# GpSimd's semaphore waits for VectorE extended to the additions of token sums and weights

## The chip, the cores and the metric

One core of one Trainium2 chip runs the kernel. The metric is the device time of one execution in microseconds (us). The engines are TensorE (PE, with PEld for its weight loads), VectorE (DVE), ScalarE (ACT), GpSimd (POOL) and SyncE (SP), which issues nearly all DMAs.

## The reference

Attention with a mask, followed by two dense layers (all fp32):

```python
q_bucket = hash(q @ proj > 0); k_bucket = hash(k @ proj > 0)      # 6 bits each
mask   = q_bucket[:, None] == k_bucket[None, :]
scores = where(mask, q @ k.T / sqrt(64), -1e9)                    # batch 2, 8 heads, 768 tokens
attn   = exp(scores - max); attn = attn / (sum(attn) + 1e-9)
x = (attn @ v).transpose(...).reshape(1536, 512)
x = mish(x @ w_in1) @ w_out1                                      # 512 -> 2048 -> 512
h = x @ w_in2
out = (h - tanh(h)) @ w_out2
```

The four weight arrays come as float64 words and are converted to fp32 on the chip.

## The kernel before

**Precision.** Each fp32 matrix is split into a high and a low fp32r part (a copy, then a subtraction), and a product is three products of the parts. A large share of the work on ScalarE, VectorE and GpSimd is this splitting.

**Attention** takes about the first 230 us. It goes over eight pairs of heads; a pair has four rounds (two heads, two halves of the tokens) of six column chunks. Per round TensorE makes scores into PSUM, VectorE takes the minimum and clamps (line 672), ScalarE makes the exponential (line 694), TensorE transposes the weights back into PSUM (lines 734 and 736), and each transposed chunk is split into `ph` and `pl`: most by ScalarE and VectorE straight from PSUM (lines 757 and 763), some by GpSimd from a copy that ScalarE puts into SBUF (line 749; lines 750 and 753, the former shown in the profile as line 421, the helper `pool_copy`). TensorE then multiplies by the values (lines 706 and 709). Beside this run, for the next pair, the splitting of q, k and v (lines 472, 503 and 627, with the copies on line 421) on GpSimd, the hash bits on VectorE (line 508, two halves in each pair), and the DMAs that stack operands. `finish` (lines 822 to 829) scales the result of a pair and puts it into `xh` and `xl`.

**Dense layers.** Each is eight units of 256 hidden columns over two blocks of tokens. Most units use a seven-product block scheme (Strassen's kind) that needs sums and differences of token blocks (`tokens`) and of weight blocks. For the first block the raw sums are made of attention's results in the fp32 tiles that the results were written to; the differences among them are made by `diff` (line 1026), on VectorE, and can run during attention, as soon as two pairs are finished. The weights of the first two units are converted during attention as well (`to_float`: lines 954 and 962 on VectorE, line 970 on ScalarE, line 974 on GpSimd).

**Order of issue.** Every instruction group is an `op` with an engine, a cost and a key. `Plan.order` (lines 235 on) simulates the engines with these costs and sorts all groups by their planned start; the program is written out in that order, and each engine executes its own instructions in order. The planner counts a VectorE group as `inside` when its cost is over 0.3 and none of its buffers lies in PSUM (line 231). It never plans such a group beside a GpSimd group. When the program is written out, a semaphore wait repeats a part of this on the chip:

```python
    holders = []                                                   # line 1547
    for o in plan.order():
        made = o.fn()
        if o.eng == "DVE" and plan.inside(o) and made is not None:
            holders.append(made)
        elif o.eng == "POOL" and made is not None:
            for h in holders[-1:]:
                tc.add_manual_dep(made.ins, h.ins.name, ..., reason="port")
            holders.clear()
```

So a GpSimd group waits for the last `inside` VectorE group written out since the GpSimd group before it, if that VectorE group's function returned its instruction. The functions for lines 954 and 962 do. Those that call `add` (line 919; its instruction is line 920) return nothing, since `add` returns nothing. `add` makes the token differences (line 1026), the low parts of the split token blocks (1037) and weights (1113 and 1119), the weight sums (1103 to 1106) and most of VectorE's work in the dense layers. GpSimd has no work after attention.

Of the kernel before, what the change touches and what calls it, by code (L numbers as in the profile page):

```python
# [32 lines left out]
ALU = mybir.AluOpType  # L33
# [288 lines left out]
def tile_lsh_attention_moe(  # L322
# [34 lines left out]
    op, buf, room = plan.op, plan.buf, plan.room  # L357
# [559 lines left out]
    dram = {}  # L917

    def add(eng, out, in0, in1, sub=False):
        eng.tensor_tensor(out=out, in0=in0, in1=in1, op=ALU.subtract if sub else ALU.add)  # L920

    def unit_at(n):
        return T_MOE + n * UNIT
# [73 lines left out]
    def tokens(layer, sb, keys, slack):  # L997
# [11 lines left out]
        for k in range(2):  # L1009
# [10 lines left out]
            def whole(name, i, key, k=k, x=x, tmp=tmp, both=both):  # L1020
                at_ = ops[name][0]
                if (layer, sb) != (1, 0):
                    op(*TOKS, key, lambda: add(et, tmp(i), at_(0, k), at_(1, k)), [*x_of(name), *gate], both(i), release=key - slack)

            def diff(i, a, b, key, x=x, tmp=tmp, both=both):
                op(*TOKS, key, lambda: add(et, tmp(i), tmp(a), tmp(b), True), [*both(a), *both(b)], both(i))

            def place(name, i, key, k=k, x=x, tmp=tmp, both=both):
                at_ = ops[name][0]
                if name == "t1":  # L1030
                    toks = x_of("b12")
                    hi, lo = toks[:HT], toks[HT:]
                else:
                    (h, l) = more[("t2", "t3", "t4").index(name)]
                    hi, lo = [(h, k)], [(l, k)]
                op("ACT", 0.38, key, lambda: nc.scalar.copy(at_(0, k), tmp(i)), [*both(i), *gate], hi)
                op("DVE", 0.48, key + 0.1, lambda: add(nc.vector, at_(1, k), tmp(i), at_(0, k), True), [*both(i), *hi], lo)
# [576 lines left out]
```

## Time and profile before

| what | value |
| --- | --- |
| median of 3 runs | 739.85 us (739.48 to 739.94) |
| profiled execution, device time | 739.25 us |
| its span, first to last instruction | 737.5 us |
| TensorE, matmuls busy | 717.1 us (97%) |
| VectorE busy | 647.6 us (88%) |
| ScalarE busy | 508.8 us (69%) |
| GpSimd busy | 181.8 us (25%) |
| mean granted TensorE clock | 0.993 |

Busy time is summed over the whole span, so the stages differ from these shares: GpSimd's 181.8 us all lie in the first 230. Times in the profile count from the first instruction of the span. "Idle before" is the time in which an engine did nothing before an instruction, and the name behind it is the instruction that ended the wait.

### The profile page before, as it was taken

To read this page: it belongs to the slowest core of one execution; us is meant where nothing else is said; L and a number is where in the kernel's file an instruction comes from. 1 tells how busy PE (TensorE), PEld (TensorE's weight loads), DVE (VectorE), ACT (ScalarE), POOL (GpSimd) and SP (SyncE) were. 2 spreads that over 40 slices of the span, in tenths; PEclk is the share of its full clock that TensorE was granted. 3 is DMA by queue.
4 is the path that set the end of the run, shared out by engine and by line. 5 is a ranking of instruction groups with operands and counts; after the bars stand their busy time and mean duration, and the time that the engine had idled before them with its cause. 6 is when DMAs were issued, how large, how long until landed. Compare 5 with 4: busy or idle time off the path is not lost.

```text
span 737.5 us, 12852 instructions
## 1 busy us (share of the span) xinstructions
PE 717.1 (97%) x4381; PEld 656.0 (89%) x4381; DVE 647.6 (88%) x1348; ACT 508.8 (69%) x1093; POOL 181.8 (25%) x245
## 2 busy tenths in 40 slices
PE   8995999999999999999999999999999999999998
PEld 5784898888888998999999999999999899999998
DVE  7999999999999999998798998789999575767883
ACT  5994898999995966676576666676666345476660
POOL 6797599989950000000000000000000000000000
PEclk9997999999999999999999999999999999999999
DMA  8884568686651665556544754999876786745621
GB/s 216 201 219 113 151 171 211 171 217 170 135 186 25 232 194 172 175 198 224 205 171 144 253 208 174 363 362 326 326 282 251 279 272 241 229 156 189 212 97 64
DMA packets 60673, 150.87 MB, mean 205 GB/s; under 512 B 7256, under 2 KB 23768, under 8 KB 60608
## 3 DMA queue, kind: packets, MB, share of 16 engines
q1 hardware_dynamic: 60320, 149.75, 62.8%
q8 instruction: 34, 0.56, 0.3%
q10 hardware_dynamic: 288, 0.30, 0.2%
q14 instruction: 31, 0.25, 0.1%
HBM read 88.19 MB, written 43.04 MB: 178 GB/s over the span
## 4 chain that ended last, share of the span: by engine, by line
PE 73%; DVE 17%; issue 4%; ACT 3%; POOL 1%; DMA 1%; SPq 0%; DVEq 0%; POOLq 0%; ACTq 0%
PE pt L1152 10%; PE pt L1154 10%; PE pt L1153 10%; PE pt L1242 6%; DVE p L672 6%; PE pt L1230 5%; PE pt L1229 5%; PE s L1229 5%; PE pt L1468 5%; PE s L1468 3%; PE s L1242 3%; DVE pl L763 2%; PE pt L736 2%; PE pt L709 2%; PE pt L706 2%
## 5 line engine op out<-in xcount | busy, mean ns | idle before, releaser
L694 ACT ACTIVATE p<-p,mn 128x768 f32<-128x768 f32 x96 | 91.1, 949 | 17.8 <-DVE p L672 15.9
L1152 PE MATMUL pt<-xh,a 128*128 128x384 f32 x280 | 94.3, 337 | 0.4 <-DVE ph L920 0.4
L1154 PE MATMUL pt<-xh,a 128*128 128x384 f32 x280 | 94.4, 337 | 0.0
L1153 PE MATMUL pt<-xl,a 128*128 128x384 f32 x280 | 94.4, 337 | 0.0
L763 DVE TENSOR_TENSOR pl<-pt,ph 128x384 fp32r<-128x384 f32 x148 | 77.4, 548 | 1.2 <-ACT ph L757 0.2
L757 ACT CAST ph<-pt 128x384 fp32r<-128x384 f32 x148 | 68.2, 486 | 8.0 <-PE pt L736 6.4
L1230 PE MATMUL pt<-gh,o 128*128 128x256 f32 x256 | 71.9, 281 | 0.0
L736 PE MATMUL pt<-idr,split 128*128 128x128 f32 x544 | 68.6, 241 | 0.2 <-DVE pl L763 0.2
L736 PEld LDWEIGHTS pt<-idr,split 128*128 128x128 f32 x544 | 62.3, 141 | 5.7 <-DVE p L672 0.4
L709 PE MATMUL pt<-pl,vt 128*64 128x384 f32 x192 | 66.2, 348 | 0.1
L706 PE MATMUL pt<-ph,vt 128*128 128x384 f32 x192 | 66.0, 345 | 0.0
L920 DVE TENSOR_TENSOR gl<-pl,gh 128x384 fp32r<-128x384 f32 x96 | 52.4, 553 | 10.1 <-ACT gh L1176 9.8
L672 DVE TENSOR_SCALAR_CACHE_REDUCE p<-s 128x768 f32<-128x768 f32 x62 | 58.7, 947 | 2.1 <-PE s L669 1.9
L668 PE MATMUL s<-b,a 128*128 128x512 f32 x124 | 45.5, 367 | 11.2 <-DVE p L672 10.9
L1152 PEld LDWEIGHTS pt<-xh,a 128*128 128x128 f32 x280 | 52.6, 188 | 3.8 <-DVE ph L920 0.7
L1153 PEld LDWEIGHTS pt<-xl,a 128*128 128x128 f32 x280 | 52.6, 188 | 1.2
L1154 PEld LDWEIGHTS pt<-xh,a 128*128 128x128 f32 x280 | 52.5, 188 | 0.0
L1176 ACT CAST gh<-pl 128x384 fp32r<-128x384 f32 x96 | 48.7, 514 | 4.7 <-DVE pl L920 3.8
L1190 ACT COPY ph<-pt 128x384 f32<-128x384 f32 x58 | 27.9, 482 | 32.7 <-PE pt L1154 32.6
L1230 PEld LDWEIGHTS pt<-gh,o 128*128 128x128 f32 x256 | 48.1, 188 | 0.0
L1229 PE MATMUL s<-gh,o 128*128 128x512 f32 x128 | 47.6, 394 | 0.0
L1229 PE MATMUL pt<-gh,o 128*128 128x512 f32 x128 | 47.6, 394 | 0.0
(333 smaller groups left out, 2149.1 us busy)
## 6 DMA issues: line engine op xcount, KB each, us to landing
w<-w SPq DMA_DIRECT2D x52, 512.0 KB
raw<-in_moe_w_in_dram SPq DMA_DIRECT2D x14, 1024.0 KB
raw<-in_moe_w_out_dram SPq DMA_DIRECT2D x14, 1024.0 KB
split<-a SPq DMA_DIRECT2D x24, 512.0 KB
a<-split SPq DMA_DIRECT2D x24, 512.0 KB
w<-raw SPq DMA_DIRECT2D x16, 512.0 KB
o<-split SPq DMA_DIRECT2D x24, 256.0 KB
b<-kh SPq DMA_DIRECT2D x30, 192.0 KB
```

What stands on the lines that cost most here:

```text
L672: nc.vector.tensor_scalar(out=out, in0=in_, scalar1=MASKED, scalar2=first, op0=ALU.min, op1=ALU.min, accum_out=low)
L694: lambda: nc.scalar.activation(out=p.tile(t), in_=p.tile(t), func=AF.Exp, bias=mn(), scale=-1.0, accum_out=sm()[:, st, h:h + 1],),
L706: nc.tensor.matmul(o()[:, :HB], vt()[:, c, :], ph()[:, :HB], start=(c == 0), stop=(c == NT - 1), skip_group_check=True)
L709: nc.tensor.matmul(o()[:D, :HB], vt()[:, c, :D], pl()[:, :HB], start=False, stop=False, skip_group_check=True)
L736: nc.tensor.transpose(pt()[:, t * P:(t + 1) * P].bitcast(F32R), ps.turned(t, c), idr)
L757: op("ACT", 0.376, key + AT_H, lambda: nc.scalar.copy(ph()[:, w], pt()[:, :HB]), both, [ph])
L763: nc.vector.tensor_tensor(out=pl()[:, w], in0=pt()[:, :HB], in1=ph()[:, w], op=ALU.subtract)
L1152: nc.tensor.matmul(o, tl()[:, 0, c], at_(0, kk), start=start and kk == 0, stop=False, skip_group_check=not start)
L1153: nc.tensor.matmul(o, tl()[:, 0, c], at_(1, kk), start=False, stop=False, skip_group_check=not start)
L1154: nc.tensor.matmul(o, tl()[:, 1, c], at_(0, kk), start=False, stop=kk == 1, skip_group_check=not start)
L1229: nc.tensor.matmul(a()[:, n, :], w()[:, y, c], flat[x][:, :SEG], start=st, stop=sp)
L1230: nc.tensor.matmul(r()[:, 0, rest], w()[:, y, c], flat[x][:, SEG:], start=st and d % 2 == 0, stop=sp, skip_group_check=True)
```

## The change

`add` returns the instruction that it makes. So the lambdas that call it return it too, and where such a group is `inside`, it enters `holders`.

```diff
     def add(eng, out, in0, in1, sub=False):
-        eng.tensor_tensor(out=out, in0=in0, in1=in1, op=ALU.subtract if sub else ALU.add)
+        return eng.tensor_tensor(out=out, in0=in0, in1=in1, op=ALU.subtract if sub else ALU.add)
```

The order of issue stays as it is. In that order, six GpSimd groups have one or more `inside` groups made by `add` in front of them and get a wait for the last of these; none of the six had a wait of this kind before:

| VectorE addition waited for (start in the trace) | GpSimd group that waits |
| --- | --- |
| token difference, line 1026, `pl<-ph,pl` (60.49) | conversion addition, line 974 |
| token difference, line 1026, `t<-t` (96.67) | high part of a chunk, line 750 |
| token difference, line 1026, `ph<-ph` (148.43) | high part of a chunk, line 750 |
| token difference, line 1026, `ph<-ph,pl` (200.02) | high part of a chunk, line 750 |
| low part of a weight tile, line 1113, `a<-w,a` (206.16) | high part of a chunk, line 750 |
| low part of a weight tile, line 1119, `o<-w,o` (226.19) | high part of a chunk, line 750 |

## Rows read from the trace of the kernel before

**Rows 1.** The page: busy tenths of TensorE in 40 slices of the span.

```profile
PE   8995999999999999999999999999999999999998
```

**Rows 2.** Chain that ended last, in order of time: start us, us, what.

```profile
60.49 9.15 DVE pl L920
69.64 0.89 DVE p L672 x2
```

**Rows 3.** Waits from 60 to 76 us: total us, times, longest us.

```profile
PE s L668 <- DVE p L672: 8.6, 1, 8.6
...
DVE p L672 <- PE s L669: 0.7, 1, 0.7
```

**Rows 4.** Line 920, 0 to 235 us: count, ns min/median/max, first and last start.

```profile
L920 DVE TENSOR_TENSOR a<-w,a x2: 681/791/901, 206.2 to 220.4; 128x512 fp32r<-128x512 f32 x2
L920 DVE TENSOR_TENSOR o<-w,o x2: 680/681/682, 226.2 to 231.1; 128x512 fp32r<-128x512 f32 x2
...
L920 DVE TENSOR_TENSOR t<-t x1: 564/564/564, 96.7 to 96.7; 128x384 f32<-128x384 f32 x1
L920 DVE TENSOR_TENSOR ph<-ph,pl x1: 549/549/549, 200.0 to 200.0; 128x384 f32<-128x384 f32 x1
```

**Rows 5.** GpSimd's timeline, 59 to 80 us: start us, us, what.

```profile
59.82 0.98 POOL L472 TENSOR_SCALAR q<-q 128x384 f32<-128x384 f32 x2
60.78 1.29 POOL L974 TENSOR_TENSOR w<-w,raw 128x512 uint32<-128x512 uint32 x1
...
67.30 1.93 POOL L503 TENSOR_TENSOR kl<-k,kh 128x384 fp32r<-128x384 f32 x2
79.72 0.51 POOL L421 TENSOR_SCALAR ph<-f 128x384 fp32r<-128x384 f32 x1 [10.49 <-ACT f L749]
```

**Rows 6.** Timeline of VectorE and GpSimd around 148, 208 and 228 us.

```profile
147.70 1.32 POOL L974 TENSOR_TENSOR w<-w,raw 128x512 uint32<-128x512 uint32 x1
...
148.43 1.48 DVE L920 TENSOR_TENSOR ph<-ph 128x384 f32<-128x384 f32 x1
148.97 0.52 POOL L421 TENSOR_SCALAR ph<-f 128x384 fp32r<-128x384 f32 x1
149.74 0.53 POOL L421 TENSOR_SCALAR vt<-v 128x384 fp32r<-128x384 f32 x1 [0.25 <-PE pt L706]
...
208.00 0.51 POOL L421 TENSOR_SCALAR ph<-f 128x384 fp32r<-128x384 f32 x1 [2.92 <-ACT f L749]
...
227.57 0.51 POOL L421 TENSOR_SCALAR ph<-f 128x384 fp32r<-128x384 f32 x1 [6.79 <-ACT f L749]
```

**Rows 7.** Stretches: length, busy us by engine (instructions), granted clock, DMA share, GB/s.

```profile
69.64:76.00 6.36, 5.42 (x21) 4.75 (x22) 5.19 (x17) 3.17 (x7) 0.00 (x0) 0.52 0.01 1
...
96.67:148.43 51.76, 50.87 (x361) 44.46 (x360) 50.76 (x131) 48.17 (x113) 49.08 (x65) 1.00 0.73 194
...
60.78:97.57 36.79, 28.20 (x185) 24.88 (x184) 34.54 (x67) 24.53 (x59) 23.92 (x33) 0.86 0.52 129
69.64:96.67 27.03, 26.09 (x168) 23.23 (x169) 24.78 (x66) 22.30 (x52) 14.57 (x19) 0.89 0.48 120
```

The busy columns are TensorE, its weight loads, VectorE, ScalarE, GpSimd.

**Rows 8.** Timeline of VectorE and GpSimd around 92 us.

```profile
92.06 0.67 DVE L962 SCALAR_TENSOR_TENSOR w<-raw,w 128x512 uint32<-128x512 uint32 x1
...
92.89 1.01 POOL L829 TENSOR_TENSOR xl<-t,xh 128x384 fp32r<-128x384 f32 x1 [1.08 <-DVE w L962]
```

**Rows 9.** VectorE's timeline: first half of hash bits of three pairs.

```profile
50.73 0.66 DVE L508 TENSOR_SCALAR z<-pt,cst 56x384 fp32r<-56x384 f32 x1
...
86.31 0.67 DVE L508 TENSOR_SCALAR z<-pt,cst 56x384 fp32r<-56x384 f32 x1
...
189.39 0.66 DVE L508 TENSOR_SCALAR z<-pt,cst 56x384 fp32r<-56x384 f32 x1
```

**Rows 10.** Conversions on VectorE, lines 954 and 962, 0 to 232 us.

```profile
L954 DVE TENSOR_SCALAR w<-raw x8: 417/424/998, 9.6 to 180.4; 128x512 uint32<-128x512 uint32 x8
...
L962 DVE SCALAR_TENSOR_TENSOR w<-raw,w x8: 671/719/1330, 21.9 to 187.0; 128x512 uint32<-128x512 uint32 x8
```

## The prediction
> **What bounds the kernel now.** I read the page's forty slices first. TensorE is at nine tenths or more in nearly all of them, but the fourth slice (55 to 74 us) has a 5 [rows 1]. So the kernel is bound by the steady work of its engines, with one hole. Next, the chain of work that ended last shows what fills the hole: one VectorE addition of token sums (line 920) that takes 9.15 us, from 60.49 to 69.64, and right behind it on the chain the next VectorE minimum [rows 2]. The list of waits says who stood still for it: TensorE 8.6 us, for the VectorE instruction queued behind the addition [rows 3]. A line-by-line look at line 920 gives the same operation, 128x384, at 564 and 549 ns elsewhere [rows 4]. So some 8.6 us of the 9.15 are not work.
>
> What holds it? GpSimd's timeline [rows 5]: two instructions until 60.80, then eleven more from 60.78 to 69.23 with no gap (the first and the last stand there), and then a pause of 10.49 us. The addition ends 0.41 us after GpSimd's last instruction. The same pattern stands at 148.43: an addition of 1.48 us meets a GpSimd instruction that ends at 149.02, a second runs to 149.49, then GpSimd pauses 0.25 us for TensorE, and the addition ends at 149.91, 0.42 us after that second instruction [rows 6]. I read this so: an addition with both inputs in SBUF can't proceed while GpSimd has instructions one behind another, and it needs 0.41 us once GpSimd has stopped.
>
> The Trainium skill (SBUF — State Buffer, "Summary: rules for kernel authors") says that of two such instructions the second to issue blocks until the first finishes. Taken by the letter, that is one GpSimd instruction, so the addition would have ended about 61.2, nothing would be left for this change to save, and the rest of the 9.15 us would have another cause. The eleven instructions speak against that reading; it is the third case below.
>
> **The change, part by part.** It removes, adds and moves no computation, no DMA and nothing on SP's queue. It adds six waits on GpSimd. The first is the one that counts: the conversion addition of line 974, the first of the eleven [rows 5].
>
> 1. *The addition at 60.49.* The two instructions ahead on GpSimd are not held, so it still waits to 60.80; then the next GpSimd instruction waits for it. With the 0.41 us it ends at 61.21: 0.72 us in place of 9.15. On the path, since TensorE and ScalarE wait behind VectorE: **-8.43 us**. The other bound is the free duration, 0.55: -8.60.
>
> 2. *The slow clock behind the stall.* From 69.64 to 76.00 the granted clock averages 0.52, that is 1.2 of 2.4 GHz nearly throughout, after 8.6 us in which TensorE waited [rows 3, 7]. VectorE then waits for TensorE's scores (0.7 us) [rows 3]. From 69.64 to 96.67 VectorE is busy 24.78 of 27.03 us, so 2.25 idle; from 96.67 to 148.43, with the clock at 1.00, it is idle 1.00 of 51.76, a share of 1.9%, which would be 0.5 us here [rows 7]. The difference: **-1.7 us**. Bounds: 0 and -2.25.
>
> 3. *The addition at 148.43.* The wait is set on the GpSimd copy that starts at 148.97. The addition then ends at 149.02 + 0.42 = 149.44 and not at 149.91: **-0.5 us**; bounds 0 and -0.93 (down to the free 0.55).
>
> 4. *The other four waits.* At 96.67 and 200.02 the additions take their free time [rows 4]. The two weight splits, 0.68 us from 206.16 and from 226.19, end well before the GpSimd copies behind them (208.00 and 227.57), which wait for ScalarE [rows 4, 6]. I cost them at nothing; the cover is ScalarE's copy, and if it came early, GpSimd would wait up to 0.68 us each.
>
> 5. *What GpSimd pays.* Behind a waited-for VectorE operation GpSimd starts 0.16 us after its end: 92.06 + 0.67 = 92.73, then 92.89 [rows 8]. So line 974 starts at 61.37 in place of 60.78, 0.59 us late, and behind it in the queue the hi/lo splits of two transposed chunks, the values and the next keys; their takers are TensorE's products and the stack DMAs. And GpSimd loses its cover: until now it drained its queue while the others stood still. From 60.78 to 97.57 it is busy 23.92 us [rows 7]. Starting at 61.37 it gets through that by 85.3, and by 86.4 with the 1.08 us it waits for VectorE at 92.89 [rows 8]. VectorE gets to the same point at 61.21 + 24.78 + 0.5 = 86.5. So the two arrive together, GpSimd without slack: what is late next is GpSimd. It runs as full (49.08 of 51.76 us) from 96.67 to 148.43, where VectorE idles 1.9% [rows 7], so I take a small cost, **+0.4 us**; bounds 0 and 1.7 (the 0.59, and 1.1 more if it is as late again as its wait of 1.08).
>
> Sum: -8.43 - 1.7 - 0.5 + 0.4 = **-10.2 us**. A second way checks it: VectorE makes the hash bits of each head pair once; the first of them start at 50.73, 86.31 and, four pairs on, 189.39 [rows 9]. A pair takes (189.39 - 86.31)/4 = 25.8 us, the one with the stall 35.6, an excess of 9.8. After the change 0.17 us of excess is left in the addition; with the 0.5 at 148.43 that is a gain of 10.1.
>
> Does it reach the end? After attention TensorE is full in every slice to the end [rows 1], and everything there (weight loads included) is started by events of this chain, not by a time. So I carry the gain through whole. The profiled execution took 739.25 us (span 737.5, 1.75 around it), the median of the runs is 739.85, 0.60 more. 739.25 - 10.2 + 0.60 = 729.65, so **729.7 us**.
>
> **Rivals.**
> - *GpSimd becomes the bound.* It has no slack after 61 us, and a late queue there delays products and the next pair's keys. For: the tie of step 5. Against: the next 50 us run as full. If step 2 gives nothing and step 5 its upper end: -8.43 - 0.5 + 1.7 = -7.2; with 1.1 us more in each of the next pairs some -5. About 733 to 735.
> - *The stall moves and multiplies (slower).* The wait is set only on the next GpSimd instruction in the written order. If GpSimd lags VectorE, every VectorE operation with two SBUF inputs waits for GpSimd's instructions still ahead of it. From 61 us on ten conversion operations (lines 954 and 962) and five additions could pay. If each paid one more of GpSimd's longest instructions, 1.32 us [rows 6], that is +19.8 - 10.2, near 749.5; it turns slower beyond 10.2/15 = 0.7 us each. Against: the 16 conversions, whose waits exist already, took at most 0.998 and 1.330 us, against 0.417 and 0.671 at the least [rows 10], although GpSimd was nearly as full.
> - *The addition is slow for a cause of its own,* or the rule by the letter holds, or the wait isn't set because the operation isn't counted. Then the 9.15 us stay. GpSimd would start line 974 at 69.80 in place of 60.78, run its 8.45 us to 78.25 and still be ready before 79.72, where it resumes now [rows 5]: no change, 739.9. Against: both long additions end 0.41 to 0.42 us after GpSimd stops.
>
> **How the numbers follow.** My forecast 0.84; GpSimd as the bound 0.08; no change 0.05; the stall multiplied 0.03. The range joins the bounds: the low end takes -8.6, -2.25 and -0.93 with step 5 at nothing (-11.8, 728.1), which needs all of them at once, so 728.3; the high end takes steps 1 and 3 and step 5's upper end (-7.2, 732.6), and I stop at 732.4. A measurement of this kernel tells about 0.2%, 1.5 us, from no change. Faster: 0.84 + 0.08 = 0.92; same 0.05; slower 0.03.
>
> **What would show it.** Step 1: the addition near 60.5 us takes 0.6 to 0.9 us and line 974 starts 0.1 to 0.2 us after it, listed as waiting for VectorE. Step 2: the granted clock stays at 1.0 from 60 to 80 us, TensorE's wait of 8.6 us is gone, and the first hash bits of the pair come near 76 us in place of 86.31. Step 3: the addition now at 148.43 falls near 138 and takes about 1.0 us. Step 4: no new pause of GpSimd at the other four. Step 5: GpSimd's pause of 10.49 us is gone; if I am wrong there, TensorE's products or VectorE wait for GpSimd between 62 and 90 us. Wrong altogether: an addition that stays long although GpSimd waits, or another VectorE operation of several us.

## The result, and the profile of the changed kernel

The changed kernel took **729.47 us** (median of 4 runs, 728.85 to 730.26) beside 739.66 for the kernel before (4 runs, 738.77 to 739.94): a ratio of 0.986, 95% interval 0.9844 to 0.9876. The forecast was 729.7 in a range of 728.3 to 732.4. The changed kernel's profiled execution is the slowest of its four: 730.26 us with a span of 728.4, since everything up to the first addition ran 1.77 us later in it than in the trace before. Times in the two traces are therefore compared from the start of the first addition.

One thing has to be said ahead, or later numbers can't be understood: the kernel before does not always stall. On the chips of the experiments 28 of its 86 executions ended between 728.05 and 732.74 us (median 729.2) and 58 between 737.95 and 741.91; with the four above, 62 of 90 are in the upper group (median 739.6), and none lies between. The changed kernel's eight executions, in two sets of runs, are all between 727.88 and 730.26. So the change takes 10 us from the executions that stall, and from the others at most the half microsecond of the third addition, which no median here resolves. Over all 90 executions that is some 7 us each (62/90 of 10.4, the distance between the two medians).

The page of the changed kernel: TensorE by slices, which answers to [rows 1].

```profile
PE   7999999999999999999999999999999999999998
```

The 5 in the fourth slice is gone. The waits from 60 to 76 us, as in [rows 3] (total us, times, longest us):

```profile
POOL w L974 <- DVE pl L920: 0.5, 1, 0.5
...
PE s L668 <- DVE p L672: 0.2, 1, 0.2
```

TensorE's 8.6 us are 0.2, and GpSimd has a new wait of 0.5, the one that the change put there. The timeline of VectorE and GpSimd around it, as in [rows 5] (start us, us, what):

```profile
61.57 1.00 POOL L472 TENSOR_SCALAR q<-q 128x384 f32<-128x384 f32 x2
...
62.26 0.71 DVE L920 TENSOR_TENSOR pl<-ph,pl 128x384 f32<-128x384 f32 x1
...
63.05 1.30 POOL L974 TENSOR_TENSOR w<-w,raw 128x512 uint32<-128x512 uint32 x1 [0.49 <-DVE pl L920]
```

The addition takes 0.71 us in place of 9.15, and line 974 starts right behind it. The stretches from the first of the six additions to the second and on to the third, as in [rows 7] (length, busy us of TensorE, weight loads, VectorE, ScalarE, GpSimd, then granted clock, DMA share, GB/s):

```profile
62.26:88.09 25.83, 25.57 (x180) 22.34 (x179) 25.31 (x66) 23.75 (x58) 23.41 (x31) 1.00 0.72 180
...
88.09:139.86 51.77, 50.87 (x361) 44.42 (x360) 50.77 (x131) 48.12 (x113) 49.06 (x65) 1.00 0.74 195
```

The first took 36.18 us before (60.49 to 96.67); it is 10.35 shorter. The second took 51.76 before and is unchanged. At the third addition, as in [rows 6]:

```profile
139.13 1.32 POOL L974 TENSOR_TENSOR w<-w,raw 128x512 uint32<-128x512 uint32 x1
...
139.86 1.01 DVE L920 TENSOR_TENSOR ph<-ph 128x384 f32<-128x384 f32 x1
```

The addition's 1.48 us have become 1.01. From the start of the first addition to the end of the span the kernel before took 737.5 - 60.49 = 677.0 us, the changed one 728.4 - 62.26 = 666.1: 10.9 less. Of these, 10.35 lie ahead of the second addition and 0.47 in the third; the 0.05 us left over is, on balance, all that is lost or won behind them, the dense layers included.

### The profile page after: what moved, and what is told of

Its sections match the earlier page's. It is cut to its first block, busy times and chain, and to the rows that moved or that the text cites. A ratio compares the mean times of both kernels' runs of the same rounds, so it can differ in the third digit from the quotient of the medians.

```text
span 728.4 us, 12853 instructions
## 1 busy us (share of the span) xinstructions
PE 714.8 (98%) x4381; PEld 654.6 (90%) x4381; DVE 637.9 (88%) x1348; ACT 507.5 (70%) x1093; POOL 183.0 (25%) x245
## 4 chain that ended last, share of the span: by engine, by line
PE 71%; DVE 19%; issue 5%; ACT 2%; POOL 2%; SPq 0%; DMA 0%; DVEq 0%; POOLq 0%; ACTq 0%
PE pt L1152 10%; PE pt L1154 10%; PE pt L1153 10%; DVE p L672 7%; PE pt L1242 6%; PE pt L1230 5%; PE pt L1229 5%; PE s L1229 5%; PE pt L1468 5%; DVE pl L763 4%; PE s L1468 3%; PE s L1242 3%; PE pt L709 1%; PE pt L706 1%; PE pt L736 1%
```

## The experiments

**Which wait counts.** The first kernel keeps only the first new wait, the second all but the first:

```diff
+    adds = itertools.count()
     for o in plan.order():
         made = o.fn()
         if o.eng == "DVE" and plan.inside(o) and made is not None:
-            holders.append(made)
+            if "add" not in o.fn.__code__.co_freevars or next(adds) == 0:   # second kernel: > 0
+                holders.append(made)
```

> Only the wait of line 974 for the first addition is kept; the other five new waits are left out. Theory (GpSimd's run of instructions holds the addition, and this one wait is nearly all of the gain): the first addition takes about 0.7 us, the third one (148.43 in the trace before) 1.48 us again; time 0.5 us over the changed kernel, about 730.0. Rival (the gain is a sum over six waits): some 1 to 8 us over it.

> The five other new waits are kept, the first is left out. Theory: the first addition takes 9.1 us again, TensorE waits 8.6 us, the granted clock falls to 1.2 GHz behind it, and the third addition takes 1.0 us; time 0.5 us under the kernel before, about 739.2. Rival (the sum over six waits): clearly under 738.

First only: 729.18 us (12 executions, 728.23 to 730.50, none in the upper group). All but the first: 738.88 (12 executions; 10 between 738.42 and 739.55, two at 728.07 and 729.32). The first and third additions of the kernel with the first wait only:

```profile
60.05 0.70 DVE L920 TENSOR_TENSOR pl<-ph,pl 128x384 f32<-128x384 f32 x1
...
137.66 1.47 DVE L920 TENSOR_TENSOR ph<-ph 128x384 f32<-128x384 f32 x1
```

And of the kernel with all but the first:

```profile
60.42 9.15 DVE L920 TENSOR_TENSOR pl<-ph,pl 128x384 f32<-128x384 f32 x1
...
148.47 1.00 DVE L920 TENSOR_TENSOR ph<-ph 128x384 f32<-128x384 f32 x1
```

The first and the third wait each do their own part, and the first is nearly all of the gain. The half microsecond of the third is seen in the traces; the medians are too coarse for it. The two low executions of the second kernel, and those of the kernel before beside it, were the first sign of the two groups.

**How long the addition is held.** The wait for the first addition is put on a later GpSimd instruction, behind three or seven others:

```diff
+    adds, skip, first = itertools.count(), 3, None      # or 7
...
+        if o.eng == "POOL" and made is not None and first is not None:
+            if not skip:
+                holders, first = [first], None
+            skip -= 1
         if o.eng == "DVE" and plan.inside(o) and made is not None:
-            holders.append(made)
+            if "add" in o.fn.__code__.co_freevars and next(adds) == 0:
+                first = made
+            else:
+                holders.append(made)
```

> The wait for the first addition is put on the fourth GpSimd instruction behind it (a low part of line 753) and not on the first; the other five waits as changed. Theory (the addition proceeds only when GpSimd stops): it ends 0.41 us after the third of those instructions, which lies 2.25 us after the start of line 974, so it takes 0.31 + 2.25 + 0.41 = 2.97 us, 2.25 longer than in the changed kernel; time 729.5 + 2.3 = 731.8 if the clock stays up, up to 0.6 more if it falls for a while. Rival (the addition needs one gap, or a cause of its own): 0.7 or 9.15 us, and 729.5 or 739.7.

> The wait for the first addition is put on the eighth GpSimd instruction behind it (a copy of the next keys). Theory: the seven instructions in front take 5.58 us, so the addition takes 0.31 + 5.58 + 0.41 = 6.3 us; time 729.5 + 5.6 = 735.1, and up to 1.7 more (736.8) for the slow clock behind the stall. If the clock costs what step 2 of the prediction says, this kernel shows a lower granted clock and some 7 us more, the one with three instructions not. Rival: 0.7 or 9.15 us.

Behind three: 8 of 10 executions between 731.93 and 734.35 (median of these 732.9), two at 728.60 and 730.37. Behind seven: 8 of 10 between 735.97 and 738.14 (median 736.5), two at 728.13 and 730.28. The eight behind seven have a mean granted clock of 0.991 to 0.995, the two others 0.998 and 1.000, and are 7.0 us over the changed kernel. So the time follows the place of the wait, and the rival causes fall. The first addition behind three instructions, and, in the second fence, the stretches of that kernel: from the first addition to the second, and four microseconds after the stall:

```profile
61.55 2.94 DVE L920 TENSOR_TENSOR pl<-ph,pl 128x384 f32<-128x384 f32 x1
```

```profile
61.55:90.74 29.19, 26.80 (x180) 23.68 (x179) 27.64 (x67) 23.83 (x57) 23.44 (x31) 0.94 0.62 159
...
66.00:68.00 2.00, 2.00 (x10) 1.81 (x8) 1.83 (x6) 0.79 (x3) 2.00 (x3) 0.51 0.76 265
68.00:70.00 2.00, 2.00 (x12) 1.78 (x10) 1.62 (x7) 1.69 (x4) 2.00 (x5) 0.63 0.03 3
```

2.94 us were expected to be 2.97. But the clock did not stay up, though the expectation for seven instructions says that behind three it would: after TensorE waited 2.4 us, it fell to 1.2 GHz for some three microseconds. From the first addition to the second this kernel takes 29.19 - 25.83 = 3.36 us more than the changed one, of which 2.94 - 0.71 = 2.23 are the addition and 1.1 what follows. With the whole stall it was 10.35, of which 8.44 the addition and 1.9 what follows. By these traces, one for each length, the stall's tail is a term of its own, and a short stall already has more than half of it.

The profiled execution behind seven is one of the two that didn't stall, and it shows how those go:

```profile
60.20 0.70 DVE L920 TENSOR_TENSOR pl<-ph,pl 128x384 f32<-128x384 f32 x1
...
60.45 1.61 POOL L974 TENSOR_TENSOR w<-w,raw 128x512 uint32<-128x512 uint32 x1
```

No wait stands between the two, yet the addition got in at the end of the second q copy, and line 974, started 60.45, took 1.61 us in place of 1.29, as GpSimd was now the one held. Call the moment at which one GpSimd instruction gives way to the next a border. The kernel before is a race at that one.

**What decides the race.** Two kernels without any new wait let the addition arrive later, by one or four clears on VectorE, and a third by two:

```diff
...
     for o in plan.order():
+        if o.eng == "DVE" and plan.inside(o) and "add" in o.fn.__code__.co_freevars and next(adds) == 0:
+            for _ in range(1):                          # or 4, or 2
+                nc.vector.memset(even[:, :8], 0.0)
         made = o.fn()
```

> The kernel before (no new wait), with one clear of 128x8 (0.07 us) on VectorE right ahead of the first addition, so that it reaches VectorE's head about 0.1 us later, still inside the second of the two GpSimd instructions ahead of it. The executions of the kernel before fall into two groups, near 729 and near 739.5; in the traces the group is decided by whether the first addition gets in at the first border between GpSimd instructions. Theory A (it gets in when it arrives in the last 0.1 to 0.2 us before a border, and loses when it comes earlier): nearly all executions near 729. Theory B (chance at the first border, whatever the arrival): again a quarter to a third near 729, the rest near 739.5.

> As the one with one clear, but with four, so that the addition arrives 0.3 to 0.4 us later, after GpSimd's conversion addition (1.29 us) has begun. Theory A: it comes about 1.1 us ahead of the next border, loses that and all after it; all executions near 739.7 and the addition about 8.8 us. Theory B: a quarter to a third near 730, the rest near 739.5.

> The kernel before with two clears of 128x8 on VectorE ahead of the first addition. With one clear the addition started only 0.02 us later against GpSimd's copies, with four 0.42 us, so two should give 0.1 to 0.2 us: it comes to VectorE's head within 0.1 us of the border between the second copy and line 974, as the addition at 96.67 does, which got in at its border in every trace. Theory A (an arrival close before the border gets in): nearly all executions near 729.3, the first addition about 0.6 us. Theory B (chance whatever the arrival): a third near 729, the rest near 739.5.

One clear: three executions at 739.36 to 739.69, one at 730.92; by the trace the addition had moved only 0.02 us against the copies, so this one tells little. Four clears: three at 740.24 to 740.63 (the addition 8.74 us in the trace, expected 8.8), one at 732.43, where theory A had all four stall. Two clears: 9 of 11 between 738.23 and 742.15, two at 728.57 and 729.02. VectorE and GpSimd with two clears, by a trace that stalled:

```profile
60.37 8.98 DVE L920 TENSOR_TENSOR pl<-ph,pl 128x384 f32<-128x384 f32 x1
...
60.47 1.31 POOL L974 TENSOR_TENSOR w<-w,raw 128x512 uint32<-128x512 uint32 x1
```

The addition came 0.1 us ahead of the border, and lost more often than not. Theory A falls. The next kernel moves GpSimd's border instead:

```diff
...
+        if i == late:                                   # ahead of the two copies of q
+            for _ in range(2):
+                nc.gpsimd.memset(even[:, 70:71], 0.0)
         made = o.fn()
```

> The kernel before with two clears of 128x1 (0.1 us each) on GpSimd ahead of the two copies in front of line 974, so that the border comes about 0.2 us later and the addition 0.4 us ahead of it, as the one at 148.43 does, which lost its first border in every trace without a wait. Theory A: all executions near 739.5, the addition about 9.3 us. Theory B: a third near 729, the rest near 739.5.

All 11 executions between 728.04 and 730.88, median 729.0, ratio 0.9901 (0.9861 to 0.9941), the opposite of what was expected. GpSimd and VectorE in its trace:

```profile
59.95 1.39 POOL L472 TENSOR_SCALAR q<-q 128x384 f32<-128x384 f32 x2
...
60.42 0.55 DVE L920 TENSOR_TENSOR pl<-ph,pl 128x384 f32<-128x384 f32 x1
```

The expectation had counted to the wrong border. With the copies 0.2 us later, the addition starts 0.47 us into the first copy, whose length is 0.5, so it arrives at the border between the two copies. It takes its free 0.55 us, and the second copy is the one held (the pair takes 1.39 in place of 0.98). The second of the six additions meets its pair of copies nearly so: 0.09 to 0.13 us ahead of the second copy, and it takes 0.55 to 0.56 us in all 14 traces. In the kernel before:

```profile
96.29 1.31 POOL L472 TENSOR_SCALAR q<-q 128x384 f32<-128x384 f32 x2
...
96.67 0.56 DVE L920 TENSOR_TENSOR t<-t 128x384 f32<-128x384 f32 x1
```

Is it that border, or the moment? The last kernel puts line 974 ahead of the two copies, so that an addition already held meets the border between them:

```diff
...
+    todo.insert(to, todo.pop(conv))                     # line 974 ahead of the two copies of q
```

> The kernel before, with GpSimd's line 974 moved ahead of the two copies of q, so that the first addition arrives inside line 974, some 0.5 us ahead of its end, and the first border it meets is that from line 974 to a copy, as at 148.43; the border between the two q copies comes next, when the addition has been waiting for a while. Theory C1 (the kind of border decides; that between the two q copies lets an addition in, as in every trace at 96.67 and in the kernel with the border later): the addition takes 1.5 to 1.8 us and nearly all executions are near 730.5. Theory C2 (an addition gets in surely only when it arrives at a border, and one that has lost a border loses those behind it): the addition takes about 9 us and nearly all executions are near 739.5.

Seven of 12 executions between 738.87 and 741.47, five between 728.95 and 730.08. A traced one of the seven:

```profile
59.61 1.31 POOL L974 TENSOR_TENSOR w<-w,raw 128x512 uint32<-128x512 uint32 x1
...
60.29 9.15 DVE L920 TENSOR_TENSOR pl<-ph,pl 128x384 f32<-128x384 f32 x1
...
60.89 0.98 POOL L472 TENSOR_SCALAR q<-q 128x384 f32<-128x384 f32 x2
```

The held addition went past the border between the copies like past all others, so C1 falls for an addition that is held already. C2 holds for what comes after a lost border, but not for the first one: 5 of 12 got in, at a border that no trace shows.

What the runs support is this. An addition that arrives at the border between two copies of q takes its free time (the second addition in 14 of 14 traces, and by their times all 11 executions with the border later). One that arrives earlier in an instruction can get in at the next border (the first addition of the kernel before, in 28 of 90 executions) or lose it (in the other 62; and the third addition, 0.54 to 0.57 us ahead of its border, in all 7 traces without its wait). One that missed its border stayed held until GpSimd had to wait, in all six traces of a stall of the first addition. Against that last rule stands one execution of the kernel before, 732.74 us, with a mean granted clock of 0.995, which otherwise only kernels with a shorter stall show (the wait behind three or seven). It has no trace, but an addition let in at a later border would look like that.

What settles a single border was not found. With two clears the first addition starts as close to its border (0.10 us) as the second does to its own, and stalled in 9 of 11 executions, while the second never did. The two borders differ in kind, copy to line 974 and copy to copy, and C1 is excluded only for an addition that is held already. The moments may differ too: the VectorE instruction in front of the second addition ends only 0.01 to 0.04 us ahead of that border, the clear in front of the first ended 0.16 us ahead of its own. No run separates the two.

**GpSimd's slack.** The changed kernel again, and with one GpSimd instruction behind the first addition repeated, to the same result, by 3 and by 1:

```diff
...
+        if extra and o.eng == "POOL" and o.fn.__code__.co_firstlineno == 627:
+            while extra:                                # 3, or 1
+                o.fn()
+                extra -= 1
```

> The changed kernel again, beside the others on this chip. Theory (the wait makes the border certain): every execution near 729.4, none near 739. Rival (the wait only shifts the odds): some near 739.

> The changed kernel, with GpSimd's low part of the values (line 627, 1.01 us) that follows the first addition made four times in place of once, same result: 3 us more work for GpSimd where step 5 of the prediction says that it has no slack. If GpSimd is level with VectorE there, the time rises by 2 to 3 us (731.4 to 732.4). If it has slack, by under 0.5 us.

> The changed kernel, with line 627 behind the first addition made twice in place of once: 1.0 us more for GpSimd. With 3 us more the time rose by 3.5 us against the changed kernel on the same chip. If GpSimd has no slack at all there, +1.0 (about 729.5 on that chip); if the tie of step 5 leaves it some, under +0.5.

The changed kernel: 728.39 (727.88 to 729.91). With the other kernels that keep the first wait where the change put it, 34 of 34 executions have no stall. With 3 us more: 731.90 (730.67 to 732.33), 3.5 over it on the same chip. With 1 us more, on another chip: 728.87 (728.31 to 730.67), which no median can tell from the 729.0 and 729.2 of kernels without it on that chip. In its trace GpSimd works 1.08 us longer and the first stretch is 26.49 us (59.71 to 86.20) against 25.83, 0.66 more. From the waits with 3 us more, 60 to 100 us:

```profile
PE pt L709 <- POOL pl L753: 2.4, 1, 2.4
```

So GpSimd has some 0.4 us of slack there (1.08 - 0.66), by one trace, and beyond that TensorE waits for its products. That the 3 us cost more than 3 fits the clock: it is 0.94 over that stretch (59.95 to 89.72 us), having fallen after the 2.4 us wait, as it did behind three instructions. No run separates the two.

No version was faster than the changed kernel; the one with the first wait alone and the one with the border moved equal it.

## Why the prediction was right, point by point

*The hole and its cause.* Shown: the time follows the place of the wait (732.9 and 736.5 us), and the stall's length with it where a trace has it (2.94 us). The reading that an addition can't proceed while GpSimd runs without a gap was too strong. It can get in at the first border it meets. Four executions of the kernel before, and a trace of one, all stalled, and gave no hint of the other group. That the forecast was measured against four stalled executions was luck: with 62 of 90 stalling, and if executions are independent, that happens about once in four times (0.69 to the fourth power is 0.23). And the 0.2% to which the prediction trusts one measurement holds within a group only; between the groups lie 10 us.

*Step 1*, 0.72 us and -8.43: 0.71, and -8.44. Right.

*Step 2*, -1.7, with *step 5*, +0.4: together -1.3 forecast; between the first two additions 10.35 - 8.44 = 1.9 were gained beside the addition itself. The size was off by 0.6. VectorE idles 25.83 - 25.31 = 0.5 us in that stretch, as step 2 had taken it, so 0.4 of the excess is step 5: line 974 starts 0.08 us behind the addition and not 0.16, GpSimd loses 0.5 us there, and this cost nothing that shows, as it has some slack that the tie denied it. The other 0.2 is VectorE's busy time there, 25.31 - 0.71 = 24.60 in place of 24.78. The tie itself was close, as 3 us more work cost 3.5. The clock is 1.00 over that stretch, as said.

*Step 3*, -0.5: 1.48 to 1.01, -0.47. Right.

*Step 4*, nothing: one of the four shows a new pause, the copy at 191.72 us, which waits 0.77 us for the fourth addition. It waited 0.60 us for ScalarE before, so it is 0.17 later; no time follows from it.

*The whole gain reaches the end*: 10.35 + 0.47 = 10.82 of the 10.9 us between the two traces, counted from the first addition. Right. The 10.2 forecast and the 10.2 between the medians agree more closely than the steps do: the traces, free of the start, give 0.7 more.

*The rivals.* GpSimd as the bound did not come about, but was less than 1 us away. The stall did not multiply: the sixteen conversions on VectorE take at most 1.00 and 1.33 us, as in [rows 10]. A cause of the addition's own is excluded by the kernels with the wait moved. The Trainium skill (SBUF — State Buffer, "Summary: rules for kernel authors") has the second to issue blocked until the first finishes; the trace of the kernel before shows eleven more instructions of the other engine behind that first one, so for a run of instructions the measurement differs. The two traces in which the addition got in without a wait (0.70 and 0.69 us) go by the rule.

## What to carry to other kernels

Where two engines exclude each other, give the engine that runs without gaps a semaphore wait on each operation of the other, and look through the code for those that slip past the rule: here a helper that didn't return its instruction. A wait that lengthens one queue by half a microsecond can be cheap insurance against a stall as long as that queue. Before comparing two medians, look at every execution: a race shows as two groups, and four executions can all fall into one.

## What the runs showed of the hardware that was not expected

- The same program, with the same order on every engine, stalls in 62 of 90 executions and in 28 not. By the traces the addition is then held for 8.6 us, or for about 0.15 (0.70 - 0.55, with the wait behind seven). In traces of both outcomes it starts 0.67 to 0.71 us behind the first q copy.
- In every trace of a stall the held VectorE addition was let in only where GpSimd itself had to wait, even across a border of the kind at which a newly arrived one gets in freely (0.55 to 0.56 us for the second addition at its pair of copies in 14 of 14 traces, 9.15 for the held one past such a pair).
- TensorE's granted clock fell to 1.2 GHz after a wait of 2.4 us (0.51 from 66 to 68 us with the wait behind three), and what followed that short stall cost 1.1 us, against 1.9 after 8.6 us.
